# Rearranging the first two batches of a fused Nyström-attention and MLP kernel, and summing rows of C at full width

## The chip, the cores and the metric

The kernel runs on one core of a Trainium2 chip. The metric is the time of one execution in device microseconds (us); lower is better. Each profile also gives the *span*, from the first to the last counted instruction, some 1.7 to 1.8 us shorter than the run's time. The *granted clock* is the share of full speed that the throttle gave TensorE. A difference counts as faster or slower only from 2% on.

Engines: PE is TensorE (PEld its weight loads), DVE is VectorE, ACT is ScalarE, POOL is GpSimd, which here issues most loads.

## The reference

Inputs are q, k, v of shape (8 batches, 8 heads, 576 rows, 64), `w_in` (512, 2048), `w_out` (2048, 512), all float32. Per head, with 32 landmarks (means over 18 rows):

```python
A  = sm(q, k_lm); Bm = sm(q_lm, k_lm); C = sm(q_lm, k)     # softmaxes of scaled scores
Z  = Bm.T / (norm1(Bm) * norminf(Bm) + 1e-6)
for _ in range(6):
    Z = 2 * Z - Z @ Bm @ Z
x  = A @ Z @ C @ v                                         # heads side by side: (4608, 512)
out = square(relu(x @ w_in)) @ w_out
```

## The kernel before

It never builds x. For each batch it makes A transposed (`AT`), the small matrix `WT` from the inverse and C·v, and then G = WT·w_in. The MLP's first product is `h = G·AT` in 16 column blocks f; ScalarE applies relu (`r`), VectorE squares it (`gT`), and TensorE multiplies by `w_out` (16 matmuls of 512 columns per output tile). While the MLP of batch b runs, the attention of batch b+1 is advanced in small steps between its blocks, so TensorE always has something to do. TensorE, VectorE and ScalarE execute their instructions in the order written.

The whole first part is written by hand in that order.

```python
# batch 0: nothing to overlap with
prepare(0, ("k",));  warm(6)                 # float32 -> bf16 halves on VectorE and ScalarE
k0 = transposed("k", 0);  k1 = transposed("k", 1)
load_rest(dve(X["qkt"][:], X["qkt32"][:]))   # w_in, v, batch 1's k and q, w_out: only after this
dve(*k0);  act(*k1)                          # copies of the transposed k
segment_means(1, "k");  transposed_tail()
prepare(0, ("q",));  warm(8)
segment_means(0, "q")                        # -> diagonal blocks bd on ScalarE and VectorE
...
# the loop over batches
for b in range(B):
    if b + 2 < B:
        load_qk(b + 2, loaded[b + 2])
        load_v(b + 2, loaded[b + 2])
    ...                                      # [cut]
    late = 3 if b == 0 else 0
    for f in range(NF):                      # 16 blocks of the MLP's first product
        square = mlp_in(b, f, AT, G, gT)
        if (b, f) == (0, 2):                 # pin: batch 1's q is converted after this square
            loaded[0]["qpin"] = square
            prepare_next(1)
        advance(tiles, 3 if b % 2 == 0 else 2)
        attend((f + 1 - late) * half // (NF - late))   # steps of the next batch's attention
    ...                                      # [cut]
    while b + 1 not in R and b + 1 < B:
        advance(tiles, 6)                    # six output matmuls per round
        attend(done + 1)
```

The row sums of C, for the softmax's denominator, use the same 32-column tiles as C·v: per batch 40 matmuls of 64 columns and 40 of a single column.

```python
for lo, hi in ((0, D), (D, D + 1)):
    for a in range(4):
        nc.tensor.matmul(cv[M * a:M * a + M, qd, lo:hi], lhsT=lh[:, M * a:M * a + M], rhs=rv, ...)
```

The softmax here doesn't subtract the row's maximum and nothing guards it: scores larger than these inputs give would overflow.

Of the kernel before, what the change touches and what calls it, by code (L numbers as in the profile page):

```python
# [8 lines left out]
P = 128  # L9
# [8 lines left out]
H = 8  # L18
# [16 lines left out]
def kernel(  # L35
# [97 lines left out]
    masked = band(mask4[:], [[32, 4]], 31, -1)  # L133
    blk_bf = const.tile([P, 4, M], BF16, name="blk_bf")
    nc.vector.tensor_copy(blk_bf[:], mask4[:, :].unsqueeze(2).to_broadcast([P, 4, M]))
# [37 lines left out]
    def prepare(b: int, nms=("k", "q")):  # L173

        X = loaded[b]
        for nm in nms:
            X[nm] = loads.tile([P, NC4, H, D], BF16, tag=nm + "nat", bufs=1, name="nat")
            X[nm + "T"] = attn.tile([P, NC4, NPAIR, P], BF16, tag=nm + "T", name="T")
            raw = X[nm + "raw"].rearrange("p h c d -> p c h d")
            if b == 0:  # L180
                for lo, hi in ((0, H // 2), (H // 2, H)) if nm == "q" else ((0, H),):
                    nc.vector.tensor_copy(X[nm][:, 0:2, lo:hi, :], raw[:, 0:2, lo:hi, :])
                    nc.scalar.copy(X[nm][:, 2:4, lo:hi, :], raw[:, 2:4, lo:hi, :])
                continue
            nc.vector.tensor_copy(X[nm][:], raw)  # L185
            if b >= DMA_T:
                nc.sync.dma_start_transpose(
                    X[nm + "T"].rearrange("p c a t -> p (c a) t"),
                    X[nm].rearrange("p c h d -> p (c h d)"))
        if "k" in nms:  # L190
            X["tT"] = attn.tile([P, NPAIR, P], BF16, tag="tT", name="tT")
            if b >= DMA_T:
                nc.sync.dma_start_transpose(X["tT"][:], X["qkt"].rearrange("p h d -> p (h d)"))

    def warm(n):

        z = bds[1].rearrange("p a b c -> p (a b c)")
        for _ in range(n):
            nc.tensor.matmul(idle[:, 0:2 * P], lhsT=z[:, 0:P], rhs=z[:, 0:2 * P],
                             start=True, stop=True)  # L200

    def attention(b: int, R: dict):
# [6 lines left out]
        def transposed(nm, half):  # L209
            if not first:  # L210
                tps = ntile([P, 2, NPAIR, P], BF16)[:]
            else:
                tps = psum.tile([P, 4, NPAIR, P], BF16, tag="h", bufs=2, name="tps")[:, 0:2, :, :]
            for i in range(2):
                for p in range(NPAIR):
                    nc.tensor.transpose(
                        tps[:, i, p, :],
                        X[nm][:, 2 * half + i, 2 * p:2 * p + 2, :].rearrange("p h d -> p (h d)"),
                        ident_bf[:],
                    )  # L220
            return X[nm + "T"][:, 2 * half:2 * half + 2, :, :], tps
# [12 lines left out]
        def segment_means(ti, nm):  # L234
# [5 lines left out]
            for n, (p, c) in enumerate(order):  # L240
                src = X[nm][:, c, 2 * p:2 * p + 2, :] if c < NC4 else X["qkt"][:, 2 * p:2 * p + 2, :]
                nc.tensor.matmul(  # L242
                    means[:, ti, p, :],
                    lhsT=src.rearrange("p h d -> p (h d)"),
                    rhs=seg[:, c + (ti if c == NC4 else 0), :],
                    start=(n == 0 and (first or ti == 1)), stop=(c == NC4), skip_group_check=True,
                )
# [44 lines left out]
        def stationary(src, tag):  # L292

            if first:
                if src.dtype == BF16:
                    return src
                res = newt.tile([P, 2, M], BF16, tag="U", name="U")
                nc.vector.tensor_copy(res[:], src)
                return res[:]
# [22 lines left out]
        def inverse_begin():  # L322
# [3 lines left out]
            cs = small.tile([P, 2], F32, tag="cs", name="cs")  # L326
            nc.vector.reduce_sum(cs[:], BB[:, 0, :, :], axis=AX.X)
            rows = small.tile([P, 2, M], F32, tag="rows", name="rows")
            nc.vector.transpose(rows[:], cs[:, :].unsqueeze(2).to_broadcast([P, 2, M]))
# [79 lines left out]
        ras = [small.tile([P, NC4 + 1, 4], F32, tag="ra", name="ra") for i in range(2)]  # L409
        rras = [small.tile([P, NC4 + 1, 4], F32, tag="rra", name="rra") for i in range(2)]  # L410
        parts = ((0, 3), (3, NC4 + 1)) if first else ((0, NC4 + 1),)

        def a_sums(i, part=0):
            lo, hi = parts[part]
            nc.vector.reduce_sum(ras[i][:, lo:hi, :],  # L415
                                 EA[:, i, lo:hi, :].rearrange("p c (h m) -> p c h m", m=M), axis=AX.X)
            if hi == NC4 + 1:
                nc.vector.reciprocal(rras[i][:], ras[i][:])

        def a_rows(i, part=0):  # L420
            lo, hi = parts[part]
# [3 lines left out]
                rras[i][:, lo:hi, :].unsqueeze(3).to_broadcast([P, hi - lo, 4, M]), ALU.mult)  # L425
# [13 lines left out]

        def c_values():  # L440

            cv = ntile([P, 2, D + 1])
            for qd in range(2):
                for c in range(NC4 + 1):
                    for lo, hi in ((0, D), (D, D + 1)):
                        for a in range(4):
                            h = 4 * qd + a
                            lh = EC[:, qd, c, :] if c < NC4 else ect[:, qd, :]
                            rv = (ones_bf[:] if lo else
                                  X["vm"][:, h, c, :] if c < NC4 else X["vt"][:, h, :])  # L450
                            nc.tensor.matmul(  # L451
                                cv[M * a:M * a + M, qd, lo:hi], lhsT=lh[:, M * a:M * a + M], rhs=rv,
                                start=(qd == 0 and c == 0 and lo == 0), stop=(c == NC4),
                                skip_group_check=True)
            rc2 = small.tile([P, 2], F32, tag="rc2", name="rc2")
            nc.vector.reciprocal(rc2[:], cv[:, :, D])
            nc.vector.tensor_tensor(cvb[:], cv[:, :, 0:D],
# [3 lines left out]
        if first:  # L461
            prepare(0, ("k",))
            warm(6)
            k0 = transposed("k", 0)
            k1 = transposed("k", 1)
            load_rest(dve(X["qkt"][:], X["qkt32"][:]))
            dve(*k0)
            act(*k1)
            segment_means(1, "k")
            transposed_tail()  # L470
            prepare(0, ("q",))
            warm(8)
# [3 lines left out]
            dve(*q0)  # L476
            q1 = transposed("q", 1)
            landmark_softmax()
            act(*q1)
            scores("k", 0)  # L480
            BT, ED = inverse_first(*inverse_begin())
            scores("q", 0)
            side = [[(scores, "q", 1), (a_sums, 0, 0)],
                    [(tails,), (a_sums, 1, 0)],
                    [(scores, "k", 1), (a_sums, 0, 1)],
                    [(a_sums, 1, 1), (a_rows, 0, 0), (warm, 2)],
                    [(a_rows, 0, 1), (c_values,)],
                    [(a_transposed, 0), (a_rows, 1, 0)],
                    [(a_rows, 1, 1), (warm, 2)],
                    [(a_transposed, 1)]]  # L490
        else:
            for ti, nm in ((1, "k"), (0, "q")):
                segment_means(ti, nm)
                yield
# [10 lines left out]
            if b < DMA_T:  # L505
                act(*transposed("q", 1))
                yield
                dve(*transposed("k", 0))
                yield
                act(*transposed("k", 1))  # L510
                yield
# [3 lines left out]
                    [(a_sums, 0), (scores, "k", 0)], [(scores, "k", 1), (a_rows, 0)],  # L515
                    [(a_sums, 1), (a_transposed, 0)], [(c_values,)],
                    [(a_rows, 1)], [(a_transposed, 1)]]

        def aside():
            for f, *args in side.pop(0):  # L520
                f(*args)
            if first:
                warm(2)
# [15 lines left out]
        for it in range(2):  # L539
# [6 lines left out]
            aside()  # L546
# [9 lines left out]
        last = nc.vector.tensor_copy(WT[:], wt[:])  # L556
        if b == 1:
            X["kpin"] = last
        if first:
            warm(3)  # L560
# [3 lines left out]
        for n in range(4):  # L564
            with tc.issue_after(mark[0].ins) if n == 2 and mark else nullcontext():
# [12 lines left out]
            if first:  # L578
                lo = nc.scalar.copy(dst[:, 0, :], g[0])
                last = nc.vector.tensor_copy(dst[:, 1, :], g[1])  # L580
                tc.declare_no_dep(last.ins, lo.ins, reason="other columns and banks")
                if n == 0:
                    X["kpin"] = last
# [6 lines left out]
            if n % 2:  # L590
                yield
        R[b] = (AT, G)

    mark, begin = [], []

    def mlp_in(b, f, AT, G, gT):
        o = (b % 2) * S
        h = psum.tile([P, 2, 512], F32, tag="h", bufs=2, name="h")
        for qd in range(2):
            for j in range(2):  # L600
                last = nc.tensor.matmul(h[:, j, 0:HALF], lhsT=G[:, qd, f * P:(f + 1) * P],  # L601
                                        rhs=AT[:, qd, j * HALF:(j + 1) * HALF],
                                        start=(qd == 0), stop=(qd == 1))
        if (b, f) == (0, 9):
# [54 lines left out]
    with tc.manual_schedule(engines={mybir.EngineType.PE, mybir.EngineType.DVE,  # L659
                                     mybir.EngineType.Activation}):  # L660
        for _ in attention(0, R):
            pass
    gT, tiles = None, iter(())
    for b in range(B):
# [24 lines left out]
        late = 3 if b == 0 else 0  # L689
        prepare_next(b + 1)  # L690
        for f in range(NF):
            square = mlp_in(b, f, AT, G, gT)
            if (b, f) == (0, 2):
                loaded[0]["qpin"] = square
                prepare_next(1)
            advance(tiles, 3 if b % 2 == 0 else 2)
            attend((f + 1 - late) * half // (NF - late))
# [41 lines left out]
```

## Time and profile before

| | before |
|---|---|
| median of 3 runs, us | 273.28 (273.15 to 273.67) |
| the profiled run, us / its span, us | 272.19 / 270.4 |
| mean granted clock of the profiled run | 1.000 |
| first matmul of G for batches 0, 1, 2, 7, us from the start | 23.52, 51.67, 82.38, 232.82 |

The page of the kernel before: busy time, TensorE's busy tenths in 40 slices of 6.76 us, and the chain that ended last.

```profile
PE 254.2 (94%) x3051; PEld 150.2 (56%) x3051; DVE 174.9 (65%) x497; ACT 157.6 (58%) x274; POOL 42.7 (16%) x66
PE   2978799999999999999999999999999999999994
PE 69%; DVE 15%; DMA 10%; ACT 3%; issue 1%; SPq 0%; POOL 0%; DVEq 0%
```

TensorE is nearly full from the sixth slice (33.8 us) on. What can be won is before it and a little after it, or by giving TensorE less to do.

The timeline of TensorE in batch 3's C·v stage of the kernel before. Columns: start in us, duration in us, engine, line, operation, output<-inputs, tile shape, elements, count.

```profile
109.15 0.21 PE L451 MATMUL n<-vm,EC 128*32 128x64 bf16 x4
...
109.75 0.20 PE L451 MATMUL n<-ones_bf,ect_91 128*32 128x1 bf16 x4
109.88 0.39 PE L630 MATMUL ops_2185<-w_out_bf,gT 128*128 128x512 bf16 x1
```

Durations overlap, so cost is read from start to start: 80 matmuls from 109.15 to 109.88, 0.73 us.

Batch 0's chain in the kernel before, lines of the timelines of ScalarE, VectorE and TensorE, in this order; brackets give the idle time before a line and what ended it.

```profile
8.96 1.01 ACT L468 COPY T<-tps 128x1024 bf16<-128x1024 bf16 x1 [1.63 <-PE tps L216]
11.89 0.26 ACT L257 CAST bd_83<-n 64x128 bf16<-64x128 f32 x1 [0.56 <-PE n L242]
...
19.72 0.21 DVE L298 CAST U<-n 128x64 bf16<-128x64 f32 x1
...
15.76 0.24 PE L314 MATMUL n<-EY 32*32 32x64 bf16 x8 [0.96 <-DVE EY L343]
...
23.52 0.41 PE L573 MATMUL g<-w_in_bf,WT 64*32 64x512 bf16 x8 [0.19 <-DVE WT L556]
```

The milestones are the diagonal blocks of q's means (11.89), the first product of the inverse (15.76), U in the second half of the inverse (19.72) and G (23.52).

The conversions of k and q, VectorE's timeline in the kernel before: first those of batch 1, then those of batch 2. The last line is ScalarE's first relu.

```profile
28.95 0.69 DVE L185 COPY nat<-raw 128x2048 bf16<-128x2048 bf16 x1 [0.64 <-DMA raw<-in_k_dram]
31.66 0.69 DVE L185 COPY nat<-raw 128x2048 bf16<-128x2048 bf16 x1 [0.91 <-DMA raw<-in_q_dram]
...
51.47 0.68 DVE L185 COPY nat<-raw 128x2048 bf16<-128x2048 bf16 x1
...
53.82 0.68 DVE L185 COPY nat<-raw 128x2048 bf16<-128x2048 bf16 x1
...
25.34 0.65 ACT L607 ACTIVATE r<-h 128x576 bf16<-128x576 f32 x1 [0.27 <-PE h L601]
```

Batch 1's conversions wait for their loads.

### The profile page before, as it was taken

To read this page: it belongs to the slowest core of one execution; us is meant where nothing else is said; L and a number is where in the kernel's file an instruction comes from. 1 tells how busy PE (TensorE), PEld (TensorE's weight loads), DVE (VectorE), ACT (ScalarE), POOL (GpSimd) and SP (SyncE) were. 2 spreads that over 40 slices of the span, in tenths; PEclk is the share of its full clock that TensorE was granted. 3 is DMA by queue.
4 is the path that set the end of the run, shared out by engine and by line. 5 is a ranking of instruction groups with operands and counts; after the bars stand their busy time and mean duration, and the time that the engine had idled before them with its cause. 6 is when DMAs were issued, how large, how long until landed. Compare 5 with 4: busy or idle time off the path is not lost.

```text
span 270.4 us, 7294 instructions
## 1 busy us (share of the span) xinstructions
PE 254.2 (94%) x3051; PEld 150.2 (56%) x3051; DVE 174.9 (65%) x497; ACT 157.6 (58%) x274; POOL 42.7 (16%) x66
## 2 busy tenths in 40 slices
PE   2978799999999999999999999999999999999994
PEld 1844565466654665556644665466645665466444
DVE  4687788758794569647974669548964859545100
ACT  2555687366935677267926676467836674577211
POOL 3744333310420202202220220200000000000000
PEclk9999999999999999999999999999999999999999
DMA  7999999999699979997599929994821011211032
GB/s 207 229 203 198 203 205 190 209 207 144 83 160 123 186 107 137 199 159 105 113 157 153 177 61 155 174 149 80 176 61 62 18 41 41 78 41 40 19 98 79
DMA packets 69793, 35.34 MB, mean 131 GB/s; under 512 B 37376, under 2 KB 64256, under 8 KB 69760
## 3 DMA queue, kind: packets, MB, share of 16 engines
q0 software_dynamic: 37696, 17.17, 54.5%
q1 hardware_dynamic: 26816, 8.39, 22.4%
q10 hardware_dynamic: 5248, 9.31, 11.3%
q8 instruction: 24, 0.39, 0.6%
q14 instruction: 9, 0.07, 0.1%
HBM read 36.70 MB, written 9.44 MB: 171 GB/s over the span
## 4 chain that ended last, share of the span: by engine, by line
PE 69%; DVE 15%; DMA 10%; ACT 3%; issue 1%; SPq 0%; POOL 0%; DVEq 0%
PE ops L630 21%; PE h L601 16%; PE n L630 9%; DMA raw<-in_q_dram 6%; DVE gT L608 4%; PE g L573 3%; DMA vm<-in_v_dram 3%; DVE ra L415 2%; PE n L314 2%; DMA qkt_94<-in_q_dram 2%; ACT r L607 2%; PE n L451 2%; PE n L242 2%; PE n L390 1%; DVE an L422 1%; PE n L432 1%
## 5 line engine op out<-in xcount | busy, mean ns | idle before, releaser
L607 ACT ACTIVATE r<-h 128x576 bf16<-128x576 f32 x128 | 81.9, 652 | 33.4 <-PE h L601 30.4
L601 PE MATMUL h<-AT,G 128*128 128x288 bf16 x512 | 83.1, 286 | 1.2 <-ACT r L607 0.8
L630 PE MATMUL ops<-w_out_bf,gT 128*128 128x512 bf16 x304 | 83.2, 379 | 0.1
L608 DVE TENSOR_TENSOR gT<-r 128x576 bf16<-128x576 bf16 x128 | 57.4, 452 | 39.2 <-ACT r L607 38.1
L630 PEld LDWEIGHTS <-gT 128*128 128x128 bf16 x592 | 53.6, 98 | 40.5 <-issue 6.4
L601 PEld LDWEIGHTS <-G 128*128 128x128 bf16 x512 | 45.5, 97 | 21.6 <-issue 2.4
L630 PE MATMUL n<-w_out_bf,gT 128*128 128x512 bf16 x112 | 29.6, 380 | 0.0
L587 DVE CAST G<-g 128x1024 bf16<-128x1024 f32 x14 | 17.1, 1225 | 13.2 <-PE g L573 13.2
L585 ACT CAST G<-g 128x1024 bf16<-128x1024 f32 x14 | 14.2, 1012 | 9.5 <-PE g L573 9.1
L639 ACT COPY o_sb<-ops 128x512 f32<-128x512 f32 x19 | 11.1, 585 | 4.5 <-PE ops L630 4.4
L436 ACT COPY AT<-n 128x576 bf16<-128x576 bf16 x9 | 5.7, 638 | 13.5 <-PE n L432 11.1
L314 PEld LDWEIGHTS <-ED 128*128 128x128 bf16 x84 | 6.7, 97 | 12.2 <-DVE ED L305 8.4
L390 PEld LDWEIGHTS <-T 128*128 128x128 bf16 x256 | 11.3, 98 | 3.7
L422 DVE TENSOR_TENSOR an<-EA,rra 128x640 bf16<-128x640 f32 (+2 forms) x18 | 13.3, 740 | 0.0
L415 DVE TENSOR_REDUCE ra<-EA 128x20 f32<-128x640 f32 (+2 forms) x18 | 13.0, 721 | 0.0
L84 POOL DMA_DIRECT2D qkt<-in_k_dram x7 | 4.8, 690 | 46.7 <-PE n L252 30.1
L106 POOL DMA_DIRECT2D vm<-in_v_dram x8 | 7.1, 881 | 32.1 <-PE n L451 27.4
L242 PEld LDWEIGHTS <-nat 128*128 128x128 bf16 x256 | 8.7, 97 | 5.1 <-DVE nat L185 2.3
L96 POOL DMA_DIRECT2D raw<-in_k_dram x7 | 6.6, 936 | 29.3 <-DVE ED L305 18.6
L394 ACT ACTIVATE EA<-n 128x512 f32<-128x512 f32 x16 | 9.7, 607 | 1.8 <-PE n L390 1.8
L185 DVE COPY nat<-raw 128x2048 bf16<-128x2048 bf16 x14 | 9.4, 686 | 1.6 <-DMA raw<-in_q_dram 0.9
L394 ACT ACTIVATE EC<-n 128x512 bf16<-128x512 f32 x16 | 9.7, 604 | 1.2 <-PE n L390 1.1
(185 smaller groups left out, 322.6 us busy)
## 6 DMA issues: line engine op xcount, KB each, us to landing
out_dram<-o_sb ACTq DMA_DIRECT2D x31, 256.0 KB, 4.0
vm<-in_v_dram POOLq DMA_DIRECT2D x8, 512.0 KB, 14.7
raw<-in_k_dram POOLq DMA_DIRECT2D x7, 512.0 KB, 10.5
raw<-in_q_dram POOLq DMA_DIRECT2D x7, 512.0 KB, 13.8
w_in_bf<-in_moe_w_in_dram POOLq DMA_DIRECT2D x4, 512.0 KB, 10.2
w_out_bf<-in_moe_w_out_dram POOLq DMA_DIRECT2D x4, 512.0 KB, 16.2
out_dram<-o_sb ACTq DMA_DIRECT2D x9, 128.0 KB, 2.4
raw<-in_k_dram SPq DMA_DIRECT2D x1, 1024.0 KB, 5.5
```

Source lines behind the costliest of these rows:

```text
L242: nc.tensor.matmul(means[:, ti, p, :], lhsT=src.rearrange("p h d -> p (h d)"), rhs=seg[:, c + (ti if c == NC4 else 0), :], start=(n == 0 a ...
L314: nc.tensor.matmul(res[a:a + w, qd, :], lhsT=diagonal[a:a + w, qd, :], rhs=moving(qd)[a:a + w], start=True, stop=True)
L390: nc.tensor.matmul(sc[:, c, j, :, :], lhsT=X[nm + "T"][:, c, p, :], rhs=BD[:, 1 if nm == "q" else 0, p, 0:64], start=True, stop=True)
L394: nc.scalar.activation((EA if nm == "q" else EC)[:, qd, 0:NC4, :], sc.rearrange("p c j i m -> p c (j i m)"), AF.Exp, scale=SCALE)
L415: nc.vector.reduce_sum(ras[i][:, lo:hi, :], EA[:, i, lo:hi, :].rearrange("p c (h m) -> p c h m", m=M), axis=AX.X)
L422: nc.vector.tensor_tensor(an[:, i, lo:hi, :].rearrange("p c (h m) -> p c h m", m=M), EA[:, i, lo:hi, :].rearrange("p c (h m) -> p c h m", ...
L585: nc.scalar.copy(dst, gg[:])
L587: last = nc.vector.tensor_copy(dst, gg[:])
L601: last = nc.tensor.matmul(h[:, j, 0:HALF], lhsT=G[:, qd, f * P:(f + 1) * P], rhs=AT[:, qd, j * HALF:(j + 1) * HALF], start=(qd == 0), stop ...
L607: nc.scalar.activation(r.rearrange("p (j t) -> p j t", j=2), h[:, :, 0:HALF], AF.Relu)
L608: return nc.vector.tensor_tensor(gT[:, f, o:o + S], r[:], r[:], ALU.mult)
L630: mark[:] = [nc.tensor.matmul(ops, lhsT=gT[:, f, t * P:t * P + P], rhs=w_out_bf[:, f, i * n:i * n + n], start=(f == 0), stop=(f == NF - 1))]
```

## The change

Its intent: shorten batch 0's chain by splitting its VectorE and ScalarE work into small pieces, start batch 0's MLP on the first half of G while the second half is still to be made, place batch 1's conversions and k transposes where its loads land, and take the row sums of C in 10 full-width matmuls in place of 40 narrow ones.

The core of the diff. Cuts are marked [...]; the comments after # are added here.

```diff
+                    X["cast"] = nc.scalar.copy(X[nm][:, 2:4, lo:hi, :], raw[:, 2:4, lo:hi, :])
 [...]
-                nc.vector.tensor_copy(res[:], src)            # U of the first batch's inverse
+                nc.scalar.copy(res[:], src)
 [...]                                                          # column sums of B: one float32 matmul
             for qd in range(2):
                 for c in range(NC4 + 1):
-                    for lo, hi in ((0, D), (D, D + 1)):
-                        for a in range(4): ...                 # values and ones, 32-column tiles
+                    for a in range(4): ...                     # values only
+            for qd in range(2):
+                for c in range(NC4 + 1):
+                    nc.tensor.matmul(cv[:, qd, D:D + 1], lhsT=c_of(qd, c), rhs=ones_bf[:],
+                                     start=False, stop=(c == NC4), skip_group_check=True)
 [...]
             prepare(0, ("k",))
-            warm(6)
+            load_rest(X["cast"])
+            warm(3)                                             # 512 columns each, were 256
             k0 = transposed("k", 0)
             k1 = transposed("k", 1)
-            load_rest(dve(X["qkt"][:], X["qkt32"][:]))
-            dve(*k0)
-            act(*k1)
+            dve(X["qkt"][:], X["qkt32"][:])
+            kept = dve(*k0)
+            prepare(0, ("q",), ((0, H // 2),))
             segment_means(1, "k")
+            prepare(0, ("q",), ((H // 2, H),))
             transposed_tail()
-            prepare(0, ("q",))
-            warm(8)
+            warm(3)
 [...]                                                          # k1 and q0 copied after the softmax
+            if b == 1:                                          # k transposes ahead of q's means
+                for half, evac in ((0, dve), (1, act)):
+                    evac(*transposed("k", half))
+                    yield
+            segment_means(0, "q")
 [...]
+            if first and n == 0 or n == 3:
+                R[b] = (AT, G)
-            if n % 2:
+            if n % 2 or first and n == 2:
                 yield
-        R[b] = (AT, G)
 [...]
-        late = 3 if b == 0 else 0
+        early = [0, 0, 0, 0, 0, 0, 1, 2, 3, 3, 4, 5, 7, 9, 12, half]
-            if (b, f) == (0, 2):
-                loaded[0]["qpin"] = square
+            if b == 0 and f in (4, 8):
+                loaded[0][("kpin", "qpin")[f // 8]] = square
                 prepare_next(1)
+            if (b, f) in ((0, 1), (0, 3)):
+                advance(start, 1)                               # second half of batch 0's G
-            attend((f + 1 - late) * half // (NF - late))
+            attend(early[f] if b == 0 else (f + 1) * half // NF)
```

## The prediction

> **What bounds the kernel now.** TensorE. The busy table gives it 94% of a 270.4 us span. Matmul records overlap, so I costed each stage with start-to-start pitches read from the timeline (a group of four MLP-in matmuls 0.49 us, an output matmul 0.216 us, a 128x32 one 0.028 us) and compared the sum with the stage's length. From 83 to 250 us the loss is about 1.2 us in all: saturated. Losses are at the ends: 24.6 us before the first MLP matmul; about 4.5 us between 24.6 and 43.6 us (batch 0's MLP beside batch 1's preparation); 0.6 us to 55 us; 0.9 us to 83 us; 4 us in the drain. Only the front can be recovered, plus any TensorE work removed.
>
> **Row sums of C.** Timeline: one batch's 80 narrow matmuls take 0.74 us, 9 ns each, because four 32-column tiles run side by side. The change removes 40 one-column matmuls and adds 10 full-width ones. The Trainium skill ("TensorE: Matmul & The Clock Gate", "Wait — 56ns, not 53.3ns?") says starts never come closer than about 25 ns; this trace has 16 full-width matmuls in 0.47 us, 29 ns each. So 10 cost about 0.28 us, and 40 value matmuls keep about 0.31 us: 0.59 instead of 0.74, some 0.15 us per batch, about 1 us over seven saturated batches. Four times fewer matmuls is not four times cheaper.
>
> **First batch's chain.** Batch 0's k-transpose copy (1.01 us on ScalarE) leaves the road to the means, so q's conversion starts earlier: 0.5 to 0.9 us gained if q's second half lands by about 10 us. The column sums move to TensorE (-0.45 us VectorE), but q's transposed copy (0.69 us) now sits inside the softmax-to-inverse chain: +0.25 us. In the second half of the inverse the VectorE pieces of 0.49 and 0.42 us that delay U and y by 0.3 to 0.6 us shrink or go to ScalarE. ScalarE then becomes the queue: U, scaled values, A copies, W, G pieces, first r. Net: the first relu moves from 25.34 us to about 24.8 us.
>
> **Second batch.** In 24.6 to 43.6 us ScalarE's 16 relus need 10.5 us but take 18, since in-order TensorE and VectorE stop for k (landing 28.9 us) and q (31.7 us). Copies placed later let ten relus run before q is needed, against seven; loads start about 1 us sooner. MLP 0 should end near 39.5 us instead of 43.3 us. But batch 1's chain starts its softmax at 36.5 to 37 us rather than at 34.7 us, and VectorE is 80 to 90% busy there: it then sets G of batch 1, estimated at 52.0 to 52.5 us against 53.8 us. So most of the won TensorE time returns as waiting for VectorE.
>
> **Sum.** 1.6 us at batch 1's G, about 1.1 us from the row sums and the A stage: 2.7 us. Predicted 270.5 us, eight in ten between 268.7 and 272.1. Faster by over 2% (below 267.8): 0.06; within 2%: 0.92; slower: 0.02.
>
> **What would show it.** First relu near 24.8 us; last relu of batch 0 near 39.5 us; the first wide G copy of batch 1 near 51.3 us (52.6 before); C-times-v groups near 0.6 us; steady pair period shorter by 0.3 us; PE clock still full.
>
> **What would make it wrong.** Batch 1's chain being less VectorE-bound than I think (gain 4 to 5 us); w_in loads, started earlier, delaying q; batch 2's raw loads now queued behind its v, landing after 53 us and stalling TensorE there; ScalarE's longer queue at the first relu; fewer warming matmuls lowering the clock.

## The result and the profile after

| | before | after |
|---|---|---|
| median, us (runs) | 273.21 (4) | 271.83 (4) |
| lowest to highest, us | 272.81 to 273.67 | 271.57 to 272.10 |
| span of the profiled run, us | 270.4 | 269.9 |
| first matmul of G, batch 0, us | 23.52 | 22.39 |
| first matmul of G, batch 1, us | 51.67 | 51.14 |
| first matmul of G, batch 2, us | 82.38 | 81.21 |
| first matmul of G, batch 7, us | 232.82 | 231.97 |

The ratio of the fast runs is 0.9949, 95% interval 0.993 to 0.9968: the same within 2%, and lower by half a percent (at full clock by about a quarter of a percent, see e5). The spans of the profiled runs differ by only 0.5 us, the medians by 1.4: the profiled run of before was the fastest of its runs. The traces explain the 0.5. A ratio here is the mean time of one kernel's fast runs over that of the other's in the same rounds, so it is not quite the ratio of the medians. All outputs are right.

The page of the kernel after, the same three parts as before.

```profile
PE 249.3 (92%) x2747; PEld 149.6 (55%) x2793; DVE 176.2 (65%) x493; ACT 159.3 (59%) x280; POOL 43.4 (16%) x66
PE   2988799979999999999999999999999999999994
PE 62%; DMA 18%; ACT 7%; DVE 6%; issue 4%; POOL 1%; ACTq 0%; DVEq 0%; POOLq 0%
```

Two slices changed: the third and, unexpectedly, the ninth (54 to 61 us), which fell from 9 to 7. In the chain of waits DMA rose from 10% to 18%. Some 45 matmul records are missing from this trace (2747 against 2793 weight loads), so counts below are taken from the program's instruction order.

TensorE's timeline in the C·v stage of batch 3, kernel after.

```profile
107.44 0.30 PE L476 MATMUL n<-vm,EC 128*32 128x64 bf16 x16
...
107.71 0.21 PE L476 MATMUL n<-vt,ect 128*32 128x64 bf16 x4
107.86 0.25 PE L482 MATMUL n<-ones_bf,EC 128*128 128x1 bf16 x4
```

Forty value matmuls take 0.30 us up to about 107.74 (the last group of four starts at 107.71 and such groups follow each other in 0.03 us). Then nothing starts until 107.86: a pause of about 0.12 us at the change from 32-column tiles to the full array. The ten sums take 0.27 us. The total is 0.69 us against 0.73. The kernel before pays such a pause too, at the end of its stage: its last sums are issued by 109.78 us, and the full-width output matmul starts at 109.88, 0.10 us later. So the pause is not new, it has moved: 0.63 us of narrow matmuls became 0.30 of values and 0.27 of sums.

Batch 0's chain after: ScalarE, VectorE and TensorE, to be read against the milestones before.

```profile
9.08 0.62 ACT L186 CAST nat<-raw 128x512 bf16<-128x512 f32 x1 [1.65 <-DMA raw<-in_q_dram]
11.89 0.26 ACT L268 CAST bd<-n 64x128 bf16<-64x128 f32 x1 [0.41 <-PE n L253]
...
18.96 0.21 ACT L309 CAST U<-n 128x64 bf16<-128x64 f32 x1
...
15.77 0.24 PE L325 MATMUL n<-EY 32*32 32x64 bf16 x8 [0.22 <-DVE EY L361]
...
22.39 0.41 PE L627 MATMUL g<-w_in_bf,WT 64*32 64x512 bf16 x8
```

The 1.01 us copy of k no longer stands in front of q's conversion on ScalarE, which starts at 9.08 as soon as q's first half has landed. Yet q's diagonal blocks appear at 11.89, as before, and the inverse's first product at 15.77, as before. The second half of the inverse gained: U at 18.96 (19.72 before), G at 22.39 (23.52 before), 1.13 us.

VectorE's conversions of batch 1 and batch 2 after, the copy of G that stands behind the last of them, and the first relu.

```profile
28.74 0.69 DVE L188 COPY nat<-raw 128x2048 bf16<-128x2048 bf16 x1
32.09 0.69 DVE L188 COPY nat<-raw 128x2048 bf16<-128x2048 bf16 x1
...
51.81 0.69 DVE L188 COPY nat<-raw 128x2048 bf16<-128x2048 bf16 x1 [0.79 <-DMA raw<-in_k_dram]
...
55.40 0.69 DVE L188 COPY nat<-raw 128x2048 bf16<-128x2048 bf16 x1 [1.76 <-DMA raw<-in_q_dram]
56.01 1.22 DVE L642 CAST G<-g 128x1024 bf16<-128x1024 f32 x1
...
24.50 0.68 ACT L663 ACTIVATE r<-h 128x576 bf16<-128x576 f32 x1
```

Batch 1's conversions no longer wait. Batch 2's now do: q's waits 1.76 us, and in VectorE's order G's last copy stands behind it, so the MLP of batch 1 stops after its first block (its second starts at 57.28 us). The last relu of batch 0 ends at 38.87 us, against 43.28 before.

The chain of waits of the kernel after, 38 to 60 us: start, length, what.

```profile
41.88 13.50 DMA raw<-in_q_dram
...
55.40 0.69 DVE nat L188
...
57.28 0.65 PE h L656 x4
```

Why does this load come later? The issues of GpSimd's loads, its timeline, first before, then after.

```profile
34.68 0.88 POOL L96 DMA_DIRECT2D raw<-in_k_dram  x1 [2.07 <-DVE gT L608]
37.19 0.88 POOL L96 DMA_DIRECT2D raw<-in_q_dram  x1 [1.62 <-DVE gT L608]
...
39.73 0.87 POOL L106 DMA_DIRECT2D vm<-in_v_dram  x1 [1.66 <-DMA w_out_bf<-in_moe_w_out_dram]
```

```profile
33.96 0.88 POOL L106 DMA_DIRECT2D vm<-in_v_dram  x1 [2.08 <-DMA w_out_bf<-in_moe_w_out_dram]
...
39.27 0.88 POOL L96 DMA_DIRECT2D raw<-in_k_dram  x1 [1.86 <-DVE BT L316]
41.88 0.88 POOL L96 DMA_DIRECT2D raw<-in_q_dram  x1 [1.73 <-DMA w_out_bf<-in_moe_w_out_dram]
```

In the source batch 2's k and q still come before its v. GpSimd is not held to the written order, and the order of issue turned around: v, then k, then q (41.88), where before it was k, q (37.19), v. What flips it is the new trigger of `load_rest`: with the old one put back in the kernel after, k and q are first again (e9). The Trainium skill, "DMA: Bandwidth & Descriptors", section "Two DMAs through the same engine are not ordered", says that within one queue of one engine descriptors start in order. These traces fit: the loads landed in the order of their issue, at 48.4 (k), 51.0 (q) and 54.7 us (v) before, at 48.0 (v), 51.8 (k) and 55.4 us (q) after. So q came 4.4 us later.

### The account

By the time batch 1's G starts, the kernel after has already done more of batch 0's output: 41 output matmuls against 33, by the program's order. An output matmul takes 0.216 us from start to start, so 8 are 1.73 us. The other matmuls before that point, warming and sums aside, are the same. From batch 2's G on both orders are even. Put on equal work, the stages compare like this; the last row is the sum.

| stage | before, us | after, us | gained by after, equal work |
|---|---|---|---|
| start to batch 0's G | 23.52 | 22.39 | +1.13 |
| to batch 1's G | 28.15 | 28.75 (less 1.73 of extra work) | +1.13 |
| to batch 2's G | 30.71 | 30.07 (plus 1.73) | -1.09 |
| to batch 7's G | 150.44 | 150.76 | -0.32 |
| to the end | 37.58 | 37.89 | -0.31 |
| span | 270.4 | 269.9 | +0.5 |

So 2.3 us were won at the front, and 1.7 us were given back in three places. The first theory, T1: the 1.09 us are the late loads of batch 2, put behind v. The rivals: the gain at the front was not real (work moved, not saved), or TensorE would have stood still there whatever the order of loads, because VectorE is late.

The two other losses have a trace of their own. Between G and the MLP, TensorE's timeline of the kernel before (batch 7) has six output matmuls.

```profile
235.33 1.47 PE L630 MATMUL n<-w_out_bf,gT 128*128 128x512 bf16 x6
```

After, there are three, and then a wait for ScalarE's copy of G.

```profile
234.48 0.82 PE L686 MATMUL n<-w_out_bf,gT 128*128 128x512 bf16 x3
235.47 0.65 PE L656 MATMUL h<-AT,G 128*128 128x288 bf16 x4 [0.17 <-ACT G L640]
```

Three times 0.216 us end at 235.13, and h starts at 235.47: 0.34 us lost by starts (the profile's 0.17 us is less because matmul records overlap). From batch 2 to batch 7 this wait occurs six times, once per batch, in the trace of after and in each of its nine relatives tried below, and never in the trace of before or of its three (e1, e2, e7). It fits the edit that sets `R[b]` before the last `yield`: the loop that hands out six output matmuls per round ends sooner. In the drain after batch 7 it is about the 0.31 us lost there. In the steady stages most of it is made up for: from batch 2's G to batch 7's the trace of e3, which has this edit, takes 150.78 us, that of e2, which has the row sums without it, 150.20; that is 0.11 us per batch, not 0.34. I take it that the three matmuls held back fill waits later in the stage; this is not tested. No run changes that edit alone, so this cause is read from the traces, not tested.

### The profile page after: what moved, and what is told of

It reads as the page before. It is cut to its first block, busy times and chain, and to the rows that moved or that the text cites. A ratio compares the mean times of both kernels' runs of the same rounds, so it can differ in the third digit from the quotient of the medians.

```text
span 269.9 us, 6741 instructions
## 1 busy us (share of the span) xinstructions
PE 249.3 (92%) x2747; PEld 149.6 (55%) x2793; DVE 176.2 (65%) x493; ACT 159.3 (59%) x280; POOL 43.4 (16%) x66
## 3 DMA queue, kind: packets, MB, share of 16 engines
q0 software_dynamic: 37696, 17.17, 54.7%
## 4 chain that ended last, share of the span: by engine, by line
PE 62%; DMA 18%; ACT 7%; DVE 6%; issue 4%; POOL 1%; ACTq 0%; DVEq 0%; POOLq 0%
PE ops L686 31%; PE h L656 15%; DMA w_out_bf<-in_moe_w_out_dram 6%; PE n L686 6%; DMA raw<-in_q_dram 5%; DMA w_in_bf<-in_moe_w_in_dram 5%; ACT r L663 3%; ACT G L640 2%; PE g L627 2%; DMA raw<-in_k_dram 2%; DVE ra L432 2%; DVE gT L664 2%; PE n L454 1%; PE n L253 1%; PE n L408 1%
## 5 line engine op out<-in xcount | busy, mean ns | idle before, releaser
L686 PE MATMUL ops<-w_out_bf,gT 128*128 128x512 bf16 (+1 forms) x451 | 114.5, 371 | 3.2 <-DMA w_out_bf<-in_moe_w_out_dram 1.0
L663 ACT ACTIVATE r<-h 128x576 bf16<-128x576 f32 x128 | 82.9, 658 | 29.3 <-PE h L656 24.6
L664 DVE TENSOR_TENSOR gT<-r 128x576 bf16<-128x576 bf16 x128 | 58.0, 454 | 32.7 <-ACT r L663 31.6
L695 ACT COPY o_sb<-ops 128x512 f32<-128x512 f32 (+1 forms) x29 | 16.7, 578 | 35.2 <-PE ops L686 35.2
L686 PE MATMUL n<-w_out_bf,gT 128*128 128x512 bf16 x98 | 28.7, 380 | 0.4 <-issue 0.2
L432 DVE TENSOR_REDUCE ra<-EA 128x20 f32<-128x640 f32 (+1 forms) x19 | 13.0, 701 | 0.4
L408 PE MATMUL n<-bd,T 128*128 128x64 bf16 x256 | 12.8, 193 | 0.1
```

The lines of the kernel that those rows point to most:

```text
L408: nc.tensor.matmul(sc[:, c, j, :, :], lhsT=X[nm + "T"][:, c, p, :], rhs=BD[:, 1 if nm == "q" else 0, p, 0:64], start=True, stop=True)
L432: nc.vector.reduce_sum(ra[:, quads, lo:hi, :], EA[:, quads, lo:hi, :].rearrange("p q c (h m) -> p q c h m", m=M), axis=AX.X)
L663: nc.scalar.activation(r.rearrange("p (j t) -> p j t", j=2), h[:, :, 0:HALF], AF.Relu)
L664: return nc.vector.tensor_tensor(gT[:, f, o:o + S], r[:], r[:], ALU.mult)
L686: mark[:] = [nc.tensor.matmul(ops, lhsT=gT[:, f, t * P:t * P + P], rhs=w_out_bf[:, f, i * n:i * n + n], start=(f == 0), stop=(f == NF - 1))]
L695: nc.scalar.copy(o_h, ops)
```

## The experiments

There were twelve runs, in three calls, each call on another chip. Their edits are shown shortened below, in part in words. Medians of the kernel before on the same chip are given beside each. One caution first: in many runs, of any of these kernels, the granted clock drops for a few microseconds near the start. The records then give a mean clock of 0.986 to 0.997 in place of 1.000, and the run may be 1 to 3 us longer; such runs are still labelled fast. In the traces every dip that ends before the run does is at 0.50 and lasts 3.41 or 6.83 us, so the records step by 3.41 us; a value between 0.50 and 1.00 below is a window that holds part of a dip. Where it matters I therefore also compare runs at full clock (0.998 and over). Clock is not the whole scatter: before's full-clock runs span 270.4 to 271.3 us over the three chips, and one of e1, the same program, 272.7.

### e1: the kernel before, again (a null test)

No edit.

> The kernel before, unchanged, as a null test and for a second trace of it. The profiled execution of before took 272.19 us, 1.0 us less than the median of its four other runs (273.21), while that of after was its fastest too (271.57). If the profile of before was only a lucky one, its second trace should have a span nearer 271.2 us, and the ratio of this run to before should be 1.000 with an interval of about 0.2%. If the two traces agree in span, the 1.4 us between the medians against 0.5 us between the spans needs another reason.

Measured: 274.27 us median of 6 (273.06 to 276.44), before 272.48, ratio 1.0063, 95% from 1.0024 to 1.0102. The same program came out 0.6% "slower", with an interval that excludes 1. The trace of this run, in windows of 2 us: window, length, busy time of each engine with its instructions, granted clock, DMA share, GB/s.

```profile
14.00:16.00 2.00, 0.56 (x16) 0.41 (x16) 1.77 (x8) 1.18 (x3) 1.19 (x2) 1.00 1.42 191
16.00:18.00 2.00, 1.24 (x26) 0.74 (x26) 1.32 (x6) 0.91 (x2) 0.69 (x1) 0.60 1.47 203
18.00:20.00 2.00, 2.00 (x33) 1.31 (x32) 1.27 (x4) 0.98 (x4) 0.94 (x2) 0.50 1.12 210
```

Behind a window in which TensorE was busy 0.56 of 2 us the clock fell to half; G of batch 0 started at 26.30 us instead of 23.52. In the profiled run of the kernel before, TensorE was busy 0.80 us in that window and the clock stayed 1.00. What follows: an interval covers the scatter of rounds on one chip, not these dips. Nor was the clock all of it, for one run of the six had a mean clock of 1.000 and still spanned 272.7 us. Differences of about half a percent have to be read from traces, stage by stage, and from the fastest runs.

### e2: the kernel before with the row sums of C at full width

```diff
-  for lo, hi in ((0, D), (D, D + 1)): ...   # values and ones in 32-column tiles
+  values in 32-column tiles, then
+  nc.tensor.matmul(cv[:, qd, D:D + 1], lhsT=c_of(qd, c), rhs=ones_bf[:], start=False, ...)
```

> The kernel before with the full-width row sums of C alone. The prediction's step: 0.15 us per batch, so about 1 us (272.2 us, ratio 0.996) and a pair period shorter by 0.3 us. The rival, read from the trace of after: the 40 value matmuls end with a pause of about 0.11 us before the first full-width matmul, so a batch's stage takes 0.69 us instead of 0.73; that is 0.04 us per batch, 0.3 us at most, not to be told from zero here (272.9 to 273.3 us, ratio 0.999 to 1.000), pair period the same within 0.15 us.

Measured: 272.20 us of 6 (271.69 to 272.46), before 272.48, ratio 0.9981 (0.9957 to 1.0006). At full clock its trace spans 270.5 us, before 270.4. From batch 2's G to batch 7's it takes 150.20 us against 150.44, 0.05 us per batch. The row sums alone are worth about 0.05 us per batch, a third of the 0.15 predicted.

### e3: the kernel after, with v of batch 2 issued after its q

```diff
+ X["rawdma"] = eng.dma_start(...)          # the load of q (the last of the two)
  load_qk(b + 2, loaded[b + 2])
- load_v(b + 2, loaded[b + 2])
+ with (tc.issue_after(loaded[2]["rawdma"].ins) if b == 0 else nullcontext()):
+     load_v(b + 2, loaded[b + 2])
```

> After, with batch 2's v queued behind its q again, as before had it. Theory: in after, q of batch 2 lands at 55.4 us because v went ahead of it, VectorE waits 1.8 us for it in program order and holds back the copy of G behind it, and TensorE, adjusted for its work, loses 1.2 us between the first G matmul of batch 1 and that of batch 2. Then this kernel gains 0.8 to 1.3 us on after (270.5 to 271.0 us, ratio to before 0.990 to 0.992), and the wait of the nat copy for q in the window 50 to 60 us goes below 0.3 us. Rival: TensorE has enough other work there and the wait is harmless: no gain, ratio 0.995.

Measured: 269.56 us of 6 (269.32 to 269.73), before 272.48, ratio 0.9887 (0.9864 to 0.991); span 267.8 us at full clock. VectorE's conversions of batch 2 in its trace:

```profile
51.08 0.68 DVE L188 COPY nat<-raw 128x2048 bf16<-128x2048 bf16 x1
...
53.12 0.68 DVE L188 COPY nat<-raw 128x2048 bf16<-128x2048 bf16 x1
```

They wait for nothing. The first matmuls of G for batches 1 and 2 on TensorE's timeline:

```profile
51.28 0.62 PE L627 MATMUL g<-w_in_bf,WT 64*32 64x512 bf16 x16
...
79.17 0.63 PE L627 MATMUL g<-w_in_bf,WT 64*32 64x512 bf16 x16
```

TensorE, VectorE and ScalarE have the same instruction order here as in the kernel after; only GpSimd's differs. From batch 1's G to batch 2's the trace takes 27.89 us against 30.07 in the kernel after, 2.2 us less, and the spans differ by 2.1 us. That is about double the 0.8 to 1.3 us expected: at equal work (27.89 plus 1.73) this stage is also 1.09 us shorter than before's 30.71. Which edit gives that part is not tested. T1 stands, and the rivals fall: the stop in the ninth slice was the order of loads, and the front's gain was real and reaches the end once nothing stops TensorE there (span 2.6 us below before's).

### e4: the kernel after, with batch 0's output begun two blocks later

```diff
-        if (b, f) == (0, 9):
+        if (b, f) == (0, 11):
             begin.append(last)
```

The kernel after has a new wait of 1.05 us at 33.47 us, where the first output matmul needs `w_out` before it has landed. This edit begins the output after two more blocks.

> After, with the first output matmul let in after the hidden block 11 instead of 9. Theory: in after TensorE stands 1.05 us before its first output matmul, which waits for w_out to land at 33.5 us, with ready work behind it; with the matmul two blocks later the stand goes, and the chain of batch 1, which waits behind it, moves up by 0.3 to 1.0 us: 270.9 to 271.5 us, ratio 0.992 to 0.994. Rival: q of batch 1 lands at about 31.7 us and its copy ends at 32.8 us, and the relus set the pace then, so what is won is lost to the next wait: ratio 0.995, and q's segment means start within 0.3 us of where they do in after (33.7 us).

Measured: 274.15 us of 6 (272.44 to 274.61), ratio 1.0045 (1.0012 to 1.0077). A miss. VectorE's conversion of batch 2's q in its trace:

```profile
56.76 0.69 DVE L188 COPY nat<-raw 128x2048 bf16<-128x2048 bf16 x1 [2.66 <-DMA raw<-in_q_dram]
```

It starts 1.36 us later than in the kernel after, but that is not shown to be the edit's doing: in the trace of e5, the kernel after again, it starts at 56.53 us and waits 2.46. Batch 1's G came at 51.27 us, no sooner than after's 51.14. TensorE was busy 4.42 of 7.72 us between 51.28 and 59 us, and the granted clock was then 0.74 from 60 to 65 us. Five of six runs show a mean clock of 0.987 to 0.994; the one at full clock took 272.44 us. So filling one wait earlier did not help as long as q came late, and the longer idle time there came with a drop of the clock.

### e5: the kernel after, again, on another chip

No edit.

> After, unchanged, beside the versions of it. In the first set two things moved together: the run with the first output matmul let in later (274.15 us) had a granted clock of 0.74 between 60 and 65 us, behind a TensorE stand in which q of batch 2 landed at 56.8 us, 1.4 us later than in the trace of after; only one of its six runs had the full clock (272.44 us). If that is the risk of after itself, after shows here too a mix: runs near 271.7 us at full clock and runs near 274 us with a clock below 0.995. If the clock dip belongs to the later output matmul, after stays at 271.5 to 272.2 us in all runs.

Measured: 272.19 us of 6 (271.37 to 273.27), before 272.73, ratio 0.9979 (0.9951 to 1.0007). At full clock its three runs took 271.37 to 271.65 us, those of before 272.15 to 272.23; the other three of after took 272.73 to 273.27 us. So at full clock the gain is 0.5 to 0.9 us, about a quarter of a percent (spans 269.7 to 269.9 against 270.4), as between the two traces. The half percent of the first medians is not repeated, and the clocks of before's runs there are not on record.

### e6: e3 with the old placement of batch 1

```diff
- k transposes between the means of k and those of q;  pins at f 4 and 8;  attend(early[f] if b == 0 else ...)
+ k transposes after q's;  pins at f 0 and 2;  attend((f + 1 - late) * half // (NF - late)), late = 3 if b == 0
```

> After with batch 2's v behind its q (269.56 us), and the placement of batch 1's copies, k transposes and attention steps as before had it. Theory: the placement let ten hidden blocks instead of seven run before q of batch 1 is needed and is worth 1.0 to 1.8 us of TensorE time by the first G matmul of batch 1: 270.6 to 271.4 us, and the last relu of batch 0 ends 2 us later than with the new placement (38.9 us in after). Rival: the loads set the pace of that stretch (w_in, k, q and w_out land one after another from 24.7 to 33.5 us) and the placement only reorders waits: within 0.5 us of 269.56 us.

Measured: 273.29 us of 6 (272.72 to 273.57), before 272.73, ratio 1.0015 (0.9998 to 1.0031). All six runs were below full clock. In its trace k's conversion waits 1.57 us and q's 0.70 us for their loads, and TensorE's windows read:

```profile
28.00:30.00 2.00, 0.42 (x6) 0.23 (x3) 1.51 (x3) 1.02 (x3) 0.96 (x2) 1.00 1.43 200
...
32.00:34.00 2.00, 2.00 (x27) 1.46 (x27) 1.92 (x5) 0.91 (x2) 0.18 (x1) 0.56 1.24 205
```

(In the kernel before TensorE was busy 1.25 us in 28 to 30 us, at full clock.) Without the new placement the whole gain is gone in these runs: TensorE stands still at batch 1's loads, and the clock dropped behind that. Two limits. No run of e6 was at full clock. But the one of 272.81 us has a mean clock of 0.994, which is one dip of 3.41 us; at half clock that costs at most 1.7 us. So, as an estimate, at least 271.1 us would remain without it, 1.5 us above e3, which ran on another chip. And k's pin is at block 0 here, where before it was at G's first copy, so this is the old placement only as near as the new front permits.

### e7: the kernel before with the new placement of batch 1

```diff
+ the reverse of e6's edit, made in the kernel before: early list, pins at f 4 and 8, k transposes after k's means
```

> The kernel before with the new placement of batch 1's copies, k transposes and attention steps alone; its first batch's chain and its row sums stay as they were, and v of batch 2 stays behind q. Theory: the placement alone gains 1.0 to 1.8 us on before (270.7 to 271.5 us at full clock), the first batch's chain with the woven G the rest up to the 2.9 us that after with v last has gained. Rival: the placement needs the earlier start of the hidden blocks, since the first batch's chain ends 1.1 us later here and the loads land at the same time: less than 0.5 us.

Measured: 271.27 us of 6 (270.73 to 272.99), before 272.73, ratio 0.9951 (0.9926 to 0.9975); its two runs at full clock span 269.0 and 269.1 us, those of before on this chip 270.4. The placement alone is worth about 1.4 us, nearly three times the 0.5 us of span that the whole change gave. Here the loads keep the order k, q, v, and the conversions of batch 2 (52.40 and 54.44 us) wait for nothing.

### e8: e3 and e4 together

> After with v behind q in batch 2 and the first output matmul two hidden blocks later, so without the TensorE stand of 0.8 us before w_out lands that the trace of after with v last still shows at 33.7 us. Theory: q's segment means are next behind it, ready at 33.3 us, so batch 1's chain moves up by 0.3 to 0.5 us and with it the end: 269.0 to 269.3 us. Rival: the relus on ScalarE set the pace there, and the first G matmul of batch 1 stays within 0.15 us of 51.28 us: 269.5 us.

Measured: 269.72 us of 5 (269.04 to 270.23), before 272.73, ratio 0.9882 (0.9862 to 0.9901). At full clock 269.04 us twice, span 267.3. With the loads in order, beginning the output later no longer hurts: batch 1's G starts at 50.54 us against 51.28 in e3. But 0.34 us of this was there already at batch 0's G (22.21 against 22.55), before the edit can act; 0.40 us is left. Whether e8 is better than e3 by the 0.5 us of the spans is not settled, for the two ran on different chips.

### e9: the kernel after with the old trigger of the loads

```diff
-            load_rest(X["cast"])
 [...]
-            dve(X["qkt"][:], X["qkt32"][:])
+            load_rest(dve(X["qkt"][:], X["qkt32"][:]))
```

> After, with the loads behind k and q let go by the conversion of the k and q tails, as before had it, instead of by the conversion of k. Building it shows that this alone puts v of batch 2 behind its q again in the queue: the new trigger is what turned the order. Two theories of what the earlier start of the loads (7.75 us against 8.44 us) is worth: if k and q of batch 1 set the pace at 28 to 33 us, the start 0.7 us later costs up to 0.7 us against after with v last (span 267.8 us at full clock), so 268.2 to 268.5 us; if the hidden blocks and relus set it, or if the loads in front of them only get in the way of q of batch 0, it is 267.5 to 267.9 us. In its trace the converted tails should start nearer 7.7 us than 8.16 us if the early load delayed them.

Measured: 270.54 us of 6 (269.94 to 271.30), before 272.75, ratio 0.9915 (0.9897 to 0.9933). The issue order is k, q, v again, and batch 1's G to batch 2's takes 27.90 us, like e3's 27.89. This is the second, independent way to mend the order, and it gives the same stage: T1 is confirmed. The converted tails start at 8.21 us here (8.16 in after), so nothing shows that the earlier loads delayed them. Its median is 1 us above e3's, and its two runs at full clock took 270.63 us; its trace has the clock at 0.50 from 24 to 26 us, and it ran on another chip, so what starting the loads earlier is worth by itself stays open.

### e10: e3 with VectorE's queue in batch 0 rearranged

Batch 0's first part had won nothing although q's conversion was freed. Theory F1: VectorE's order is to blame, for the copy of k's transposed half (0.69 us) and of the tail stand before q's halves. Theory F2: q's data arrive no earlier, so nothing in front of them matters.

```diff
-            kept = dve(*k0)                 # before q's halves
+            kept = dve(*k0)                 # after q's halves
-            transposed_tail()               # copied at once
+            tail = transposed_tail()        # copied after inverse_first
-            other = dve(*q0)                # after the softmax
+            other = dve(*q0)                # before the landmark scores
```

> After with v last, and VectorE reordered in the first batch's chain: the copy of k's transposes behind both halves of q's conversion, q's copy in the wait for the exponential, the tails' copy behind the first inverse products. Theory for why the first part of the chain won nothing (diagonal blocks of q at 11.9 us and first inverse products at 15.8 us in both traces): VectorE's own order, 0.69 us of k's copy ahead of q's conversion and 0.69 us of q's copy between softmax and inverse. Then the diagonal blocks come at 11.2 to 11.5 us and the first inverse products at 14.4 to 14.8 us, and the first G matmul at 21.2 to 21.7 us. What that is worth at the end: up to 1 us if the chain sets the pace, under 0.4 us if w_in, k and q of batch 1, landing at 24.7, 28 and 31.5 us, do (span 267.4 to 267.8 us at full clock). Rival for the first part: q's second half lands later than 10.3 us; then the diagonal blocks stay within 0.3 us of 11.9 us.

Measured: 270.17 us of 6 (269.56 to 271.23), before 272.75, ratio 0.9908 (0.9885 to 0.993). No gain on e3. VectorE's conversion of q's second half in its trace:

```profile
11.29 0.43 DVE L185 CAST nat<-raw 128x512 bf16<-128x512 f32 x1 [1.29 <-DMA raw<-in_q_dram]
```

VectorE was ready and waited 1.29 us for the load. The diagonal blocks came at 12.32 us (11.89 after) and the first product of the inverse at 15.93 us. This is F2's sign, but in this run the load landed unusually late (11.27 us; 10.38 in after, 9.94 in before), so e10 by itself shows only that the new order won nothing here. The same order in e12 tells more. There q's second half landed at 10.18 us and was converted by 10.88, and still the blocks came at 12.00. TensorE and ScalarE in e12's trace:

```profile
9.95 1.49 PE L202 MATMUL idle<-bd 128*128 128x512 bf16 x3
...
11.23 0.42 PE L255 MATMUL n<-seg,nat 128*128 128x32 bf16 x8
...
12.00 0.26 ACT L270 CAST bd<-n 64x128 bf16<-64x128 f32 x1 [1.13 <-PE n L255]
```

The three warming matmuls (`warm(3)`) stand before q's means in TensorE's order and hold them until 11.23 us. This rival, F3, was not named beforehand, and no run takes those matmuls away.

### e11: e10 and e4 together

> After with all three edits: v last, first output matmul two blocks later, VectorE reordered in the first chain. If the gains add, the span at full clock is that of v last with the later output matmul (267.3 us) less what the reordered chain gives (0 to 0.8 us): 266.5 to 267.3 us, 268.2 to 269.0 us by the clock on the wall.

Measured: 270.07 us of 6 (269.80 to 271.88), before 272.75, ratio 0.9912 (0.9889 to 0.9936). Nothing gained over e10. In its trace the clock was 0.50 from 22 to 28 us.

### e12: e11 with four more warming matmuls

```diff
-            warm(1)                         # after inverse_begin
+            warm(2)
-            (a_transposed, 0), (a_recip, 1)
+            (a_transposed, 0), (warm, 1), (a_recip, 1)
+            warm(2)                         # before the products that give WT
```

> The same with four more warming matmuls of 512 columns in the stretches where TensorE is idle most (around 14.5 and 21 us, busy 1.39 and 1.27 of 2 us in the trace of after). Theory: the dips of the granted clock in the first 30 us (0.50 to 0.70 in 2 us pieces behind such a stretch, in traces of before and of after) follow from that idleness; with the fill they become rarer, so the spread of the runs shrinks, at no cost at full clock (span within 0.2 us of the version without). Rival: the dips come at random; the share of runs below a clock of 0.996 stays at a third to a half.

Measured: 269.56 us of 4 (269.35 to 270.05), before 272.75, ratio 0.9885 (0.9864 to 0.9906). Three of its four runs were at full clock, against two of e11's six. That is what the extra matmuls were for, but four runs are too few to call it shown.

### Which version to keep

e3, e8 and e12 are the fastest: 269.56, 269.72 and 269.56 us at the median, 269.04 us as the lowest of all (e8). They are 1.1 to 1.2% below the kernel before on their own chips, under the 2% at which a difference is called faster. Among the three no order is settled. e3 is the simplest, with a spread of only 0.41 us over six runs.

## Why the prediction was right or wrong

The total was right: 270.5 us predicted, 271.83 measured, inside the range 268.7 to 272.1 but near its top. The steps under it were not all right, and that the total held is in part luck: a gain 0.7 us larger than said stood against losses of 1.1 and 1.7 us, and the range was wide.

- **TensorE is saturated from 83 to 250 us: right.** Batch 2's G to batch 7's took 150.44 us before and 150.20 to 150.78 us in the traces of e2, e3, e7 and after. Nothing could be won there beyond the row sums.
- **Row sums, 0.15 us per batch, about 1 us in all: the mis-sized term.** The C·v stage went from 0.73 to 0.69 us and e2's stages shrank by 0.05 us per batch. The costs of the matmuls themselves were right (0.27 us for the ten sums, 0.28 predicted; 0.30 us for the values, 0.31 predicted). The sum left out the pause of 0.12 us at the change of tile size, while the 0.74 us that it was compared with held before's pause of 0.10. The Trainium skill had it: "TensorEngine Tiling (Array Packing)", section "Key Properties", says "Changing tiling mode (not just tile) drains the TensorE". The floor used in the prediction ("TensorE: Matmul & The Clock Gate", "Wait — 56ns, not 53.3ns?", starts never closer than about 25 ns) agrees with ten in 0.27 us.
- **First part of batch 0's chain, 0.5 to 0.9 us: failed.** q's diagonal blocks came at 11.89 us in both traces. ScalarE was indeed freed and q's first half started 1.1 us sooner (9.08, before 10.18). But the second half, which the blocks need, ended at 11.13 on VectorE and 11.48 on ScalarE, where before it ended at 11.17 and 11.32. The prediction's condition, q's second half landing by about 10 us, was not met: it landed at 10.38 us (9.94 before). And TensorE's own order, which the step left out, held q's means behind the warming matmuls until 11.02 us (11.20 before), though q's first half was converted by 10.34. With VectorE's other work out of the way and the load in time (e12) the blocks were no earlier. How the three share the blame is not tested.
- **Column sums and q's copy, +0.25 us in the softmax-to-inverse part: right in kind, wrong in size.** They cancel: the inverse's first product is at 15.76 and 15.77 us.
- **Second half of the inverse: right, and larger than said.** All 1.13 us of the front's gain lie there. The first relu came at 24.50 us (24.8 predicted, 25.34 before).
- **Batch 1's placement: right in mechanism.** The last relu of batch 0 ended at 38.87 us (39.5 predicted, 43.28 before). The first wide copy of G of batch 1 came at 51.62 us (51.3 predicted, 52.56 before). The gain by then was 2.3 us at equal work, against 1.6 predicted; e7 shows the placement's share by itself as 1.4 us of span.
- **Batch 2's loads behind its v: named as a risk, left at no cost in the sum.** It happened just so: landing after 53 us, TensorE standing still. e3 and e9 measure it as 2.2 us of the stage; against before the stage lost 1.09. It is the largest term that the sum lacked.
- **Steady pair of batches shorter by 0.3 us: wrong in sign.** It went from 59.53 to 59.66 us between batch 3's G and batch 5's. The row sums gave 0.05 us per batch, and the new wait at the start of each MLP, which the prediction did not see in the moved `R[b]`, took more.
- **PE clock still full: right for the profiled run, not for all.** Runs below full clock occur in before and in after.

How the errors met, in the spans: 2.7 us predicted, plus 0.7 at the front (2.3 for 1.6), minus 1.1 lost at batch 2, minus 1.7 after it (0.63 lost where 1.1 was to be won), leaves some 0.5 us, as in the two traces. The total held because 2.7 us was small against the range, and because the medians differ by more than the traces.

What stays open: how much of the loss of 0.63 us after batch 2's G is the moved `R[b]` alone; what the earlier start of the loads is worth; and why the clock drops in some runs and not in others with the same TensorE share. In the traces of after and of e5 TensorE was busy 1.28 and 1.27 of 2 us between 20 and 22 us; only in e5 did the clock fall, to 0.50 between 24 and 26 us. Part of the answer is in the clock records. If their steps of 3.41 us are carried on from the edges that the records show, e5's step from 19.40 to 22.81 us holds the sparse stretch whole (TensorE busy 2.00 us); in after it is split over two steps, from 17.67 and from 21.08 us (2.93 and 2.73). Over all fourteen traces the three emptiest steps between 10 and 60 us (0.95 in e4, 1.39 in e1, 1.44 in e6) each have a dip right behind them. Between 1.85 and 2.7 us some have one and some have not, so busy time alone gives no threshold.

## What to carry to other kernels

When an edit changes what releases a group of loads, look at the order in which all loads are then issued, for a scheduler may put a transfer that nobody awaits ahead of one on which TensorE hangs; here this cost 2.2 us of trace where 2.3 us had been won. A gain at the front reaches the end only if the next thing awaited, usually a load, also comes sooner or is asked for later: shorten the chain and place its consumers together. When narrow matmuls are merged into wide ones, count the time between the two tile shapes as well as the instructions, on both sides of the comparison.

## What the Trainium skill lacked or had wrong

- "TensorEngine Tiling (Array Packing)", section "Key Properties": it says that changing the tiling mode drains TensorE, but gives no time. Here the change from 32-column tiles to the full array cost about 0.12 us between starts (107.74 to 107.86 us), as much as four 128x32 matmuls, and 0.10 us in the kernel before (109.78 to 109.88).
- "TensorE: Matmul & The Clock Gate", section "What's actually happening": it gives two states, 1.2 and 2.4 GHz, and an idle window of about 3.4 us as what throttles. Here the clock went to 0.50 behind stretches in which TensorE was never idle that long by the records: busy 0.56 of 2 us (e1), 0.42 of 2 us (e6), 1.27 of 2 us (e5). Further down, the page does tell of a kernel in which frequent short idles did the same, but it has no figure for how busy a window must be, and these runs give no threshold either. The two states agree: the dips are at 0.50 and last one or two steps of 3.41 us.
- No page that I drew on says how an issue order chosen by a scheduler can change with the release of an earlier group. Here one changed release put v's 512 KB (and its tail) ahead of k and q: q's load was issued at 41.88 instead of 37.19 us, and TensorE's stage grew by 2.2 us.
